# Dynamic convolution and tanh-shrink MLP: first weight tiles staged and cast by ScalarE, start-up taps shared anew, transposes moved

## The chip, the cores and the metric

One core of one Trainium2 chip. The metric is the device time of one execution, in microseconds (us). Every result below is a median of fast runs beside runs of the kernel before on the same chip; those runs of the kernel before had medians of 770.07 to 770.72 us. A span is the time from the first to the last instruction of the profiled execution; it is 1.8 to 2.2 us shorter than the device time. PE is TensorE's matmul pipe, PEld its weight loads, DVE is VectorE, ACT is ScalarE, POOL is GpSimd, SP is SyncE.

## The reference

```python
# x (8, 4096, 192), weight_gen (8, 4096, 8, 7)
w = softmax(weight_gen, axis=-1)                     # 7 taps for each of 8 heads
y[b, s, h, g] = sum_k w[b, s, h, k] * x_pad[b, s + k, h, g]   # x_pad: 6 zero rows ahead of each sequence
hid = y.reshape(32768, 192) @ w_in                   # w_in (192, 2048)
out = (hid - tanh(hid)) @ w_out                      # w_out (2048, 192)
```

## The kernel before

The 32,768 tokens go through in 32 superblocks of 1,024, n = 0 to 31. One superblock passes these hands:

- SP loads its weights (`wg_t`) and its rows of x (`x_t`, with a halo of six rows). There are two buffers for x, so the load of n + 3 can start only when the taps of n + 1 are done.
- ACT takes the exponential, DVE sums and inverts, and the products of x with the seven taps run on GpSimd (`products`). In superblocks 0 and 1, DVE takes four and two of them. An accumulating DMA adds the odd taps onto the even ones.
- PE transposes and sums the products through the identity (`conv`), ACT copies the result out of PSUM as `convT`.
- PE multiplies by `w_in` in 16 f tiles of 128 columns (`gemm1`), ACT takes tanh, DVE subtracts. PE multiplies the superblock before by `w_out` (`gemm2`) between the f tiles.

```python
    for k in range(K):                                    # products(n): taps
        eng, w = (nc.vector, wsm_v) if k in on_vector else (nc.gpsimd, wsm[:])
        eng.tensor_mul(dst[k]..., x_t[:, k : k + J, :]..., w[:, :, :, k : k + 1]...)
        if k == K - 2 and in_pairs:
            nc.gpsimd.dma_start(out=even..., in_=odd..., accum_op=add)
    ...
    load_wg(0); load_x(0); softmax_exp(0); softmax_norm(0, obank[0])
    load_wg(1); load_x(1)
    load_w_in(0, FA)          # GpSimd's DMA casts FP32 to BF16, lower 64 partitions
    products(0, on_vector=(3, 4, 5, 6), ..., hooks={2: rest_of_w_in})
    ...
    copy_w_in(0, FA, nc.scalar)   # to the upper 64 partitions
    copy_w_in(FA, F, nc.sync)
    products(1, on_vector=(0, 1), hooks={4: load_w_out})
    conv(0, (0, 1), (2,))
    load_x(2)
    for n in range(NTOT):
        if n + 3 < NTOT:
            load_wg(n + 3)
            load_x(n + 3)
        for p in range(J):
            gemm1(n, 2 * p); gemm1(n, 2 * p + 1)
            ...
            if n >= 1:
                gemm2((n - 1) * J + p)
            if p == 0 and 1 <= n < NTOT - 2:
                products(n + 2, behind=last_sub[0] if n > 1 else None)
            if n + 1 < NTOT:
                if p == (6 if n > 0 else 7): conv(n + 1, (0, 1))
                if p == (6 if n > 1 else 7): conv(n + 1, (2,))
```

The softmax here doesn't subtract the row's maximum and nothing guards it: scores larger than these inputs give would overflow.

## Time and profile before

770.57 us (770.43 to 771.18), span 768.7.

| kernel before | us |
|---|---|
| GpSimd's first tap of superblock 1 | 20.59 |
| first tanh of n = 0 / 1 / 2 | 22.35 / 45.11 / 71.03 |
| from there to the first tanh of n = 31, a superblock | 22.80 mean, 22.63 median |
| GpSimd's own cycle | 22.64 |
| first tanh of n = 31 / end of the span | 732.28 / 768.73 |

Mean and median of PE's cycle differ because some superblocks have a stall in them. The waits of PE between 74 and 722 us show what kind; the columns are total us, how often, and the longest:

```profile
PE pc L233 <- issue: 2.8, 5, 1.7
PE obank L289 <- issue: 0.8, 1, 0.8
PE ph L257 <- issue: 0.8, 1, 0.8
```

The list has no other line for PE. "issue" means that PE had nothing to execute although nothing that the profile shows held it.

### The profile page before, as it was taken

The page shows a single profiled execution, that of the slowest core. Times are in us where ns is not written, and L with a number is a line of the kernel's source. Part 1 is how long each engine was busy: PE and PEld are TensorE (multiplying, and loading weights), DVE is VectorE, ACT ScalarE, POOL GpSimd, SP SyncE. Part 2 cuts the span into 40 slices and gives each one's busy share as a digit, 9 for nine tenths or more (in the row PEclk, how much of TensorE's full clock was granted, in tenths as well). Part 3 has the DMA queues.
Part 4 walks back from the last instruction along what each step waited for, and adds up shares of the span by engine and source line. Part 5 has one row for each costly group of instructions (what it writes and reads, how often), then busy time and mean ns, then how long its engine had stood idle before and what let it go on. Part 6 is the DMA issues. An engine that isn't in the chain of part 4 may idle for free.

```text
span 768.7 us, 32330 instructions
## 1 busy us (share of the span) xinstructions
PE 736.7 (96%) x14784; PEld 583.1 (76%) x14784; DVE 652.9 (85%) x595; ACT 640.8 (83%) x865; POOL 695.2 (90%) x290
## 2 busy tenths in 40 slices
PE   2799999999999999999999999999999999999997
PEld 2377787777777777788777777777778777787777
DVE  5987888888898888889888888888888988888883
ACT  1777878888888888888888888888888888888883
POOL 5999999999999999999999999999999999999100
PEclk9999999999999999999999999999999999999999
DMA  7823776555677555577655557765556765542412
GB/s 209 184 81 87 182 181 150 118 145 147 169 182 174 131 129 148 150 180 182 164 123 133 150 160 182 180 128 137 143 150 172 182 181 115 125 142 72 98 43 84
DMA packets 25847, 111.37 MB, mean 145 GB/s; under 512 B 4800, under 2 KB 9456, under 8 KB 21624
## 3 DMA queue, kind: packets, MB, share of 16 engines
q1 hardware_dynamic: 14688, 76.95, 29.9%
q0 software_dynamic: 10816, 31.99, 25.8%
q8 instruction: 115, 1.88, 1.0%
q10 hardware_dynamic: 208, 0.39, 0.2%
q14 instruction: 20, 0.16, 0.1%
HBM read 54.49 MB, written 25.17 MB: 104 GB/s over the span
## 4 chain that ended last, share of the span: by engine, by line
PE 93%; DVE 2%; issue 1%; POOL 1%; DMA 1%; ACT 1%; SPq 0%; POOLq 0%
PE ph L257 43%; PE obank L289 43%; PE pc L233 6%; DVE gt L269 2%; PE po L323 1%; DMA x_t<-in_x_dram 1%; POOL even L192 1%; ACT th L267 0%; ACT convT L244 0%; POOL odd L192 0%; DVE zr L151 0%; DVE zsum L145 0%; SPq L117 0%; SPq L93 0%; SPq L121 0%
## 5 line engine op out<-in xcount | busy, mean ns | idle before, releaser
L269 DVE TENSOR_TENSOR gt<-ph,th 128x1024 bf16<-128x1024 f32 x512 | 602.8, 1219 | 93.3 <-ACT th L267 92.7
L267 ACT ACTIVATE th<-ph 128x1024 f32<-128x1024 f32 x512 | 497.2, 1022 | 65.7 <-PE ph L257 64.9
L257 PE MATMUL ph<-convT,w_in 64*128 64x512 bf16 x3072 | 382.1, 378 | 7.5 <-DVE gt L269 5.0
L289 PEld LDWEIGHTS <-gt 64*128 64x128 bf16 x7936 | 345.1, 94 | 53.4 <-issue 2.5
L289 PE MATMUL obank<-w_out,gt 64*128 64x192 bf16 x7936 | 374.6, 243 | 2.9 <-issue 2.1
L192 POOL TENSOR_TENSOR even<-x_t,wsm 128x1536 bf16<-128x1536 f32 x94 | 272.8, 2903 | 3.9 <-DMA x_t<-in_x_dram 1.6
L192 POOL TENSOR_TENSOR odd<-x_t,wsm 128x1536 bf16<-128x1536 f32 x93 | 269.9, 2903 | 0.0
L257 PEld LDWEIGHTS <-w_in 64*128 64x128 bf16 x3072 | 180.1, 94 | 108.4 <-issue 11.8
L192 POOL TENSOR_TENSOR last<-x_t,wsm 128x1536 bf16<-128x1536 f32 x31 | 103.4, 3336 | 0.0
L307 ACT ACTIVATE out_sb<-obank 128x192 f32<-128x192 f32 x248 | 81.9, 330 | 10.5 <-PE obank L289 4.6
L244 ACT ACTIVATE convT<-pc 128x1024 bf16<-128x1024 f32 x64 | 48.9, 808 | 31.6 <-PE pc L233 31.5
L233 PE MATMUL pc<-ident,even 64*128 64x64 bf16 x2304 | 47.9, 192 | 2.9 <-POOL even L192 1.5
L233 PEld LDWEIGHTS <-even 64*128 64x128 bf16 x2304 | 42.7, 96 | 4.1 <-issue 2.2
L201 POOL DMA_DIRECT2D even<-odd x29 | 34.9, 1205 | 9.1 <-POOL odd L192 9.1
L163 POOL TENSOR_TENSOR wsm<-e_t,zr 128x448 f32<-128x448 f32 x30 | 41.7, 1390 | 0.0
L233 PE MATMUL pc<-ident,odd 64*128 64x64 bf16 x448 | 15.5, 198 | 13.1 <-DVE odd L192 12.8
L135 ACT ACTIVATE e_t<-wg_t 128x448 f32<-128x448 f32 x32 | 18.5, 578 | 8.2 <-DMA wg_t<-in_weight_gen_dram 8.2
L233 PE MATMUL pc<-ident,last 64*128 64x64 bf16 x768 | 23.3, 192 | 1.8 <-issue 1.7
L145 DVE TENSOR_REDUCE zsum<-e_t 128x64 f32<-128x448 f32 x32 | 19.5, 609 | 2.9 <-ACT e_t L135 2.9
L233 PEld LDWEIGHTS <-odd 64*128 64x128 bf16 x448 | 11.3, 100 | 13.6 <-DVE odd L192 12.9
L151 DVE RECIPROCAL zr<-zsum 128x64 f32<-128x64 f32 x30 | 16.6, 553 | 3.0
L233 PEld LDWEIGHTS <-last 64*128 64x128 bf16 x768 | 17.0, 96 | 2.2 <-issue 1.8
(20 smaller groups left out, 48.7 us busy)
## 6 DMA issues: line engine op xcount, KB each, us to landing
x_t<-in_x_dram SPq DMA_DIRECT2D x24, 1344.0 KB
even<-odd POOLq DMA_DIRECT2D x29, 1024.0 KB, 8.8
out_dram<-out_sb SPq DMA_DIRECT2D x31, 768.0 KB
x_t<-in_x_dram SPq DMA_DIRECT2D x8, 1176.0 KB
wg_t<-in_weight_gen_dram SPq DMA_DIRECT2D x32, 224.0 KB
x_t<-in_x_dram SPq DMA_DIRECT2D x8, 157.5 KB
w_in<-in_moe_w_in_dram POOLq DMA_DIRECT2D x6, 128.0 KB, 7.5
w_out<-in_moe_w_out_dram POOLq DMA_DIRECT2D x1, 768.0 KB, 10.8
```

The costliest lines, as they stand in the source:

```text
L135: nc.scalar.activation(out=e_t[:].rearrange("p j h k -> p (j h k)"), in_=wg_t[:].rearrange("p j h k -> p (j h k)"), func=ACT.Exp,)
L145: nc.vector.reduce_sum(out=zsum[:], in_=e_t[:].rearrange("p j h k -> p (j h) k"), axis=AX.X)
L163: return eng.tensor_mul(wsm.rearrange("p j h k -> p (j h) k"), e_t[:].rearrange("p j h k -> p (j h) k"), zr.rearrange("p (n o) -> p n o", ...
L192: eng.tensor_mul(dst[k].rearrange("p c j h g -> p j h c g"), x_t[:, k : k + J, :].rearrange("p j (h c g) -> p j h c g", h=H, c=NC), w[:, : ...
L201: nc.gpsimd.dma_start(out=even[:].rearrange("p i c j h g -> p (i c j h g)")[:, 0:ACC], in_=odd[:].rearrange("p i c j h g -> p (i c j h g)" ...
L233: nc.tensor.matmul(pc[:, r, col : col + R], lhsT=prods[c][gi][r * R : (r + 1) * R, c, 2 * j : 2 * j + 2].rearrange("p j h g -> p (j h g)") ...
L244: nc.scalar.activation(out=convT[:, c0 : c0 + nch, :].rearrange("p c (j r t) -> p r (c j) t", r=2, t=R), in_=pc[:, :, 0 : nch * JH * R].re ...
L257: nc.tensor.matmul(ph[:, r, :], lhsT=w_in[r * R : (r + 1) * R, c, f * P : (f + 1) * P], rhs=convT[r * R : (r + 1) * R, c, :], start=(c == ...
L267: last_act[0] = nc.scalar.activation(out=th[:], in_=ph_f, func=ACT.Tanh)
L269: last_sub[0] = nc.vector.tensor_sub(gt[:], ph_f, th[:])
L289: mm = nc.tensor.matmul(po[:, 0:D], lhsT=g_of[n][f][r * R : (r + 1) * R, col : col + P], rhs=w_out[r * R : (r + 1) * R, f, :], start=(r == ...
L307: last_act[0] = nc.scalar.activation(out=out_sb[:, j, :], in_=po[:, 0:D], func=ACT.Copy)
```

## The change

Its intent: start sooner, and let PE's transposes fill holes. It loads the first five f tiles of `w_in` as FP32 into both halves of the partitions and lets ACT cast them. Superblock 0's x comes without its halo first, and GpSimd gets three of its taps (the first of them needs no halo) and DVE four, two of them split so that the positions without halo come first. The scaling of superblock 1's weights moves from DVE to GpSimd, and superblock 2's norm and products go ahead of n = 0. The transposes of 1 sum up in the output banks during n = 0; from n = 1 on, five transposes are mixed behind each f tile of a second matmul, and two f tiles of the next one fill the hole behind them.

```diff
     load_wg(0)
     load_x(0)                       # now rows without halo first, halo after
+    load_wg(1)
     softmax_exp(0)
+    load_wg(2)
+    for c in range(NC):             # FA = 5 * P: 983 KB of FP32, both halves
+        for r in range(2):
+            nc.sync.dma_start(out=w_st[r * R : (r + 1) * R, c, :], in_=w_in_rows(c, 0, FA))
+    load_x(1)
+    load_w_in(FA, FB, last_exp[0])
     softmax_norm(0, obank[0])
-    load_wg(1)
-    load_x(1)
-    load_w_in(0, FA)
-    products(0, on_vector=(3, 4, 5, 6), ...)
+    products(0, taps=[(G_, 6, 0, J), (V, 5, 1, J), (V, 4, 2, J), (V, 5, 0, 1), (V, 4, 0, 2),
+                      (G_, 0, 0, J), (V, 3, 0, J), (V, 2, 0, J), (G_, 1, 0, J)], ...)
     softmax_exp(1)
+    for c in range(NC):
+        nc.scalar.activation(out=w_in[:, c, 0:FA], in_=w_st[:, c, :], func=ACT.Copy)
+    softmax_exp(2)
     ...
-                if p == (6 if n > 0 else 7):
-                    conv(n + 1, (0, 1))
+            if 1 <= n < NTOT - 1 and p == 6:
+                sums = conv_sums(n + 1, ((0, 1),), pcs)
+                gemm2((n - 1) * J + 6, between=lambda f: [next(sums, None) for _ in range(0 if f < LEAD else MIX)])
+                ...
+                gemm2((n - 1) * J + 7, 0, FILL)       # LEAD, MIX, FILL = 6, 5, 2
```

More of the change, by code (lines that the diff above doesn't have):

```diff
@@ L78 @@
     last_sub = {}
-    last_wsm = {}
+    last_exp = {}
     def order(inst, other, reason):
@@ L103, in load_x, with rows @@
         x_t = xpool.tile([P, HALO + J, D], FP32, name="x_t")
-        def rows(p0, p1):
-            win = x[b, s0 + p0 * J - HALO : s0 + p0 * J - HALO + 1]
+        def rows(p0, p1, r0=0, r1=HALO + J):
+            win = x[b, s0 + p0 * J - HALO + r0 : s0 + p0 * J - HALO + r0 + 1]
             nc.sync.dma_start(
-                out=x_t[p0:p1, :, :],
+                out=x_t[p0:p1, r0:r1, :],
                 in_=bass.AP(
@@ L111, in rows, with no_halo @@
                     offset=win.offset,
-                    ap=[[J * D, p1 - p0], [D, HALO + J], [1, D]],
+                    ap=[[J * D, p1 - p0], [D, r1 - r0], [1, D]],
                 ),
             )
-        if s == 0:
+        def no_halo():
             nc.sync.dma_start(
@@ L120, in load_x @@
             )
-            nc.sync.dma_start(
-                out=x_t[0:1, HALO : HALO + J, :],
-                in_=x[b, 0:J].rearrange("(p j) d -> p j d", p=1),
-            )
+        if n == 0:
+            rows(0, P, HALO, HALO + J)
+            rows(16, P, 0, HALO)
+            rows(1, 16, 0, HALO)
+            no_halo()
+        elif s == 0:
+            no_halo()
+            rows(0, 1, HALO, HALO + J)
             rows(1, 16)
@@ L134, in softmax_exp @@
         e_t = wgpool.tile([P, J, H, K], FP32, name="e_t")
-        nc.scalar.activation(
+        last_exp[0] = nc.scalar.activation(
             out=e_t[:].rearrange("p j h k -> p (j h k)"),
@@ L147, in softmax_norm @@
         )
+        zr = wgpool.tile([P, J * H], FP32, name="zr")
         wsm = wgpool.tile([P, J, H, K], FP32, name="wsm")
         if bank is None:
-            zr = wgpool.tile([P, J * H], FP32, name="zr")
             nc.vector.reciprocal(zr[:], zsum[:])
@@ L153, in softmax_norm @@
             return
-        zr = bank[:, 512 - J * H : 512]
-        nc.vector.reciprocal(zr, zsum[:])
+        zr_v = bank[:, 512 - J * H : 512]
         wsm_v = bank[:, 0 : J * H * K].rearrange("p (j h k) -> p j h k", j=J, h=H)
-        scale(nc.vector, wsm_v, e_t, zr)
-        last_wsm[0] = scale(nc.vector, wsm[:], e_t, zr)
-        wsm_of[n] = (wsm, wsm_v, None, None)
+        nc.vector.reciprocal(zr_v, zsum[:])
+        if n == 0:
+            scale(nc.vector, wsm[:], e_t, zr_v)
+        else:
+            nc.vector.tensor_copy(zr[:], zr_v)
+        scale(nc.vector, wsm_v, e_t, zr_v)
+        wsm_of[n] = (wsm, wsm_v, None if n == 0 else e_t, zr)
     def scale(eng, wsm, e_t, zr):
@@ L167, in scale, with products @@
         )
-    def products(n, on_vector=(), sums=None, hooks={}, behind=None):
+    def products(n, taps=None, sums=None, hooks={}, behind=None):
         x_t = x_of.pop(n)
@@ L189, in products @@
             hooks[-1]()
-        for k in range(K):
-            eng, w = (nc.vector, wsm_v) if k in on_vector else (nc.gpsimd, wsm[:])
+        for eng, k, j0, j1 in taps or [(nc.gpsimd, k, 0, J) for k in range(K)]:
+            w = wsm_v if eng is nc.vector else wsm[:]
             eng.tensor_mul(
-                dst[k].rearrange("p c j h g -> p j h c g"),
-                x_t[:, k : k + J, :].rearrange("p j (h c g) -> p j h c g", h=H, c=NC),
-                w[:, :, :, k : k + 1]
+                dst[k][:, :, j0:j1].rearrange("p c j h g -> p j h c g"),
+                x_t[:, k + j0 : k + j1, :].rearrange("p j (h c g) -> p j h c g", h=H, c=NC),
+                w[:, j0:j1, :, k : k + 1]
                 .rearrange("p j h (k o) -> p j h k o", o=1)
-                .to_broadcast([P, J, H, NC, GC]),
+                .to_broadcast([P, j1 - j0, H, NC, GC]),
             )
@@ L215, in products, with conv_sums @@
             prods_of[n] = [[dst[k] for k in (sums or range(K))]] * NC
-    def conv(n, *parts):
+    def conv_sums(n, parts, pcs, home=None):
         prods = prods_of[n]
@@ L221, in conv @@
             conv_of[n] = cpool.tile([P, NC, HT], BF16, name="convT")
-        convT = conv_of[n]
-        pcs = [psum_h.tile([P, 2, HT], FP32, name="pc", tag="ph") for _ in parts]
+        for _ in parts:
+            pcs.append(home or psum_h.tile([P, 2, HT], FP32, name="pc", tag="ph"))
+        if parts[-1][-1] == NC - 1:
+            prods_of.pop(n)
         for gi in range(max(len(g) for g in prods)):
@@ L233, in conv @@
                             nc.tensor.matmul(
-                                pc[:, r, col : col + R],
+                                pc[r][:, col : col + R] if home else pc[:, r, col : col + R],
                                 lhsT=prods[c][gi][
@@ L241, in conv, with conv_out @@
                             )
+                            yield
+    def conv_out(n, parts, pcs):
         for chunks, pc in zip(parts, pcs):
             c0, nch = chunks[0], len(chunks)
-            nc.scalar.activation(
-                out=convT[:, c0 : c0 + nch, :].rearrange("p c (j r t) -> p r (c j) t", r=2, t=R),
-                in_=pc[:, :, 0 : nch * JH * R].rearrange("p r (cj t) -> p r cj t", t=R),
-                func=ACT.Copy,
-            )
-        if parts[-1][-1] == NC - 1:
-            prods_of.pop(n)
+            out = conv_of[n][:, c0 : c0 + nch, :].rearrange("p c (j r t) -> p r (c j) t", r=2, t=R)
+            cols = nch * JH * R
+            if isinstance(pc, list):
+                for r in range(2):
+                    nc.scalar.activation(
+                        out=out[:, r],
+                        in_=pc[r][:, 0:cols].rearrange("p (cj t) -> p cj t", t=R),
+                        func=ACT.Copy,
+                    )
+            else:
+                nc.scalar.activation(
+                    out=out,
+                    in_=pc[:, :, 0:cols].rearrange("p r (cj t) -> p r cj t", t=R),
+                    func=ACT.Copy,
+                )
+    def conv(n, *parts):
+        pcs = []
+        for _ in conv_sums(n, parts, pcs):
+            pass
+        conv_out(n, parts, pcs)
     def gemm1(n, f):
@@ L266, in gemm1 @@
         g1_act[0] = last_act.get(0)
+        gt = gpool.tile([P, TOK], BF16, name=f"gt{f}", tag=f"gt{f}")
         last_act[0] = nc.scalar.activation(out=th[:], in_=ph_f, func=ACT.Tanh)
-        gt = gpool.tile([P, TOK], BF16, name=f"gt{f}", tag=f"gt{f}")
         last_sub[0] = nc.vector.tensor_sub(gt[:], ph_f, th[:])
@@ L272, with gemm2 @@
     LAST = (NTOT - 1) * J
+    LEAD, MIX, FILL = 6, 5, 2
     half = {}
     out_of = {}
-    def gemm2(i):
+    def gemm2(i, f0=0, f1=NFT, between=lambda f: None):
         ops = []
@@ L282, in gemm2 @@
             n, j = divmod(blk, J)
-            if r == 0:
+            if r == 0 and f0 == 0:
                 half[blk] = obank[blk % 2]
             ops.append((r, n, j, half[blk]))
-        for f in range(NFT):
+        for f in range(f0, f1):
             for r, n, j, po in ops:
@@ L299, in gemm2 @@
                     order(mm, g1_act[0] if i == 1 else last_act[0], "row tiles in one bank")
-        if i > 0:
+            between(f)
+        if i > 0 and f1 == NFT:
             blk = i - 1
@@ L350, in load_w_out @@
         nc.gpsimd.dma_start(out=w_out[:], in_=moe_w_out.rearrange("(c p) e -> p c e", c=NFT))
-    FA = 8 * P
-    def load_w_in(f0, f1):
-        for c in range(NC):
-            src = moe_w_in[c * GC : c * GC + 1, f0:f1]
-            dma = nc.gpsimd.dma_start(
-                out=w_in[0:R, c, f0:f1],
-                in_=bass.AP(
-                    tensor=src.tensor, offset=src.offset, ap=[[G * F, H], [F, GC], [1, f1 - f0]]
-                ),
-            )
-            if f0 == 0:
-                order(dma, last_wsm[0], "order of the loads")
@@ L368, in copy_w_in, with w_in_rows, load_w_in @@
-    def copy_w_in(f0, f1, eng):
-        eng.dma_start(out=w_in[R:P, :, f0:f1], in_=w_in[0:R, :, f0:f1])
+    FA, FB = 5 * P, 10 * P
+    w_st = const.tile([P, NC, FA], FP32, name="w_st")
+    def w_in_rows(c, f0, f1):
+        src = moe_w_in[c * GC : c * GC + 1, f0:f1]
+        return bass.AP(
+            tensor=src.tensor, offset=src.offset, ap=[[G * F, H], [F, GC], [1, f1 - f0]]
+        )
+    def load_w_in(f0, f1, behind=None):
+        for c in range(NC):
+            dma = nc.gpsimd.dma_start(out=w_in[0:R, c, f0:f1], in_=w_in_rows(c, f0, f1))
+            if c == 0 and behind is not None:
+                order(dma, behind, "order of the loads")
@@ L371, in rest_of_w_in, with copy_w_in @@
+    def copy_w_in(f0, f1):
+        nc.sync.dma_start(out=w_in[R:P, :, f0:f1], in_=w_in[0:R, :, f0:f1])
     def rest_of_w_in():
-        load_w_in(FA, F)
+        load_w_in(FB, F)
+    V, G_ = nc.vector, nc.gpsimd
     load_wg(0)
     load_x(0)
+    load_wg(1)
     softmax_exp(0)
+    load_wg(2)
+    for c in range(NC):
+        for r in range(2):
+            nc.sync.dma_start(out=w_st[r * R : (r + 1) * R, c, :], in_=w_in_rows(c, 0, FA))
+    load_x(1)
+    load_w_in(FA, FB, last_exp[0])
     softmax_norm(0, obank[0])
-    load_wg(1)
@@ L379 @@
-    load_x(1)
-    load_w_in(0, FA)
     products(
         0,
-        on_vector=(3, 4, 5, 6),
-        sums=(3, 0, 4, 5, 1, 6, 2),
-        hooks={2: rest_of_w_in},
+        taps=[
+            (G_, 6, 0, J),
+            (V, 5, 1, J),
+            (V, 4, 2, J),
+            (V, 5, 0, 1),
+            (V, 4, 0, 2),
+            (G_, 0, 0, J),
+            (V, 3, 0, J),
+            (V, 2, 0, J),
+            (G_, 1, 0, J),
+        ],
+        sums=(6, 5, 4, 3, 0, 2, 1),
+        hooks={1: rest_of_w_in},
@@ L386 @@
     )
     softmax_exp(1)
+    for c in range(NC):
+        nc.scalar.activation(out=w_in[:, c, 0:FA], in_=w_st[:, c, :], func=ACT.Copy)
+    softmax_exp(2)
     softmax_norm(1, obank[1])
-    load_wg(2)
-    copy_w_in(0, FA, nc.scalar)
-    copy_w_in(FA, F, nc.sync)
-    products(1, on_vector=(0, 1), hooks={4: load_w_out})
+    copy_w_in(FA, FB)
+    copy_w_in(FB, F)
+    products(
+        1,
+        taps=[(V, 0, 0, J), (V, 1, 0, J)] + [(G_, k, 0, J) for k in range(2, K)],
+        hooks={4: load_w_out},
+    )
@@ L393, with some @@
+    load_x(2)
+    softmax_norm(2)
+    products(2)
     conv(0, (0, 1), (2,))
-    load_x(2)
+    def some(sums, m):
+        for _ in range(m):
+            next(sums, None)
     for n in range(NTOT):
@@ L401 @@
             gemm1(n, 2 * p + 1)
-            if n == 0 and p == 1:
-                softmax_exp(2)
+            if n == 0:
+                if p == 3:
+                    pcs = []
+                    sums = conv_sums(1, ((0, 1),), pcs, obank)
+                if 3 <= p <= 6:
+                    some(sums, (3 if p == 3 else 1) * 4 * JH)
+                if p == 7:
+                    some(sums, K * 4 * JH)
+                    conv_out(1, ((0, 1),), pcs)
+                    conv(1, (2,))
+                continue
             if p == 5 and n + 3 < NTOT:
                 softmax_exp(n + 3)
-            if n >= 1:
+            if p < 6 or n == NTOT - 1:
                 gemm2((n - 1) * J + p)
-            if p == 0 and 1 <= n < NTOT - 2:
-                products(n + 2, behind=last_sub[0] if n > 1 else None)
-            if n + 1 < NTOT:
-                if p == (6 if n > 0 else 7):
-                    conv(n + 1, (0, 1))
-                if p == (6 if n > 1 else 7):
-                    conv(n + 1, (2,))
-            if n == 0 and p == 2:
-                softmax_norm(2)
-                products(2)
+            if p == 0 and n == 1:
+                softmax_exp(3)
+            if p == 1 and n == 1:
+                softmax_norm(3)
+                products(3)
+            if p == 0 and 1 < n < NTOT - 2:
+                products(n + 2, behind=last_sub[0])
+            if 1 <= n < NTOT - 1 and p == 6:
+                pcs = []
+                sums = conv_sums(n + 1, ((0, 1),), pcs)
+                gemm2(
+                    (n - 1) * J + 6,
+                    between=lambda f: [next(sums, None) for _ in range(0 if f < LEAD else MIX)],
+                )
+                for _ in sums:
+                    pass
+                conv_out(n + 1, ((0, 1),), pcs)
+                conv(n + 1, (2,))
+                gemm2((n - 1) * J + 7, 0, FILL)
             if p == 6 and n + 3 < NTOT:
                 softmax_norm(n + 3)
+            if 1 <= n < NTOT - 1 and p == 7:
+                gemm2((n - 1) * J + 7, FILL, NFT)
     gemm2(LAST)
```

## The prediction

> **What bounds the kernel now.** I first read the page (busy shares, then the chain of work that ended last), then busy time by stage, then the timelines of the start-up, of one steady superblock, and of GpSimd alone. There are 32 superblocks of 1,024 tokens, n = 0 to 31.
>
> ```profile
> PE 736.7 (96%) x14784; PEld 583.1 (76%) x14784; DVE 652.9 (85%) x595; ACT 640.8 (83%) x865; POOL 695.2 (90%) x290
> PE 93%; DVE 2%; issue 1%; POOL 1%; DMA 1%; ACT 1%; SPq 0%; POOLq 0%
> ```
>
> TensorE carries 93% of the chain that sets the end. The stages, cut at 10.3 (first tap), 20.7 (first matmul of n = 0), 44.1 (n = 1), 70.6 (n = 2) and 731.6 (n = 31):
>
> ```profile
> 10.30:20.70 10.40, 5.47 (x168) 4.68 (x169) 10.30 (x9) 1.62 (x3) 10.38 (x7) 1.00 0.74 201
> 20.70:44.10 23.40, 17.55 (x264) 8.97 (x263) 22.59 (x22) 18.31 (x21) 23.30 (x10) 1.00 0.84 206
> 44.10:70.60 26.50, 24.49 (x508) 20.48 (x509) 19.93 (x18) 20.22 (x27) 26.42 (x11) 1.00 0.25 63
> 70.60:731.60 661.00, 656.26 (x13222) 520.94 (x13223) 574.22 (x517) 577.34 (x780) 632.46 (x256) 1.00 0.59 149
> 731.60:768.70 37.10, 32.97 (x624) 28.05 (x620) 23.18 (x26) 21.46 (x35) 0.00 (x0) 1.00 0.17 66
> ```
>
> The busy columns are PE, PEld, DVE, ACT, POOL. Until 44.1 PE is not the limit: DVE and POOL are. In the steady stage PE is 99% busy, but POOL is close behind. The start-up, from the timeline:
>
> ```profile
> 10.28 1.75 DVE L192 TENSOR_TENSOR odd<-x_t,obank 128x1536 bf16<-128x1536 f32 x1 [3.77 <-DMA x_t<-in_x_dram]
> 10.32 2.90 POOL L192 TENSOR_TENSOR even<-x_t,wsm 128x1536 bf16<-128x1536 f32 x1 [1.57 <-DMA x_t<-in_x_dram]
> 18.90 1.70 POOL L358 DMA_DIRECT2D w_in<-in_moe_w_in_dram x3
> 20.59 2.93 POOL L192 TENSOR_TENSOR even<-x_t,wsm 128x1536 bf16<-128x1536 f32 x1
> 23.40 7.21 DVE L269 TENSOR_TENSOR gt<-ph,th 128x1024 bf16<-128x1024 f32 x6 [0.60 <-ACT th L267]
> 36.13 0.97 POOL L163 TENSOR_TENSOR wsm<-e_t,zr 128x448 f32<-128x448 f32 x1
> ```
>
> Both tap engines wait for x of superblock 0 until 10.3, while its weights are ready at 6.5. Then DVE needs 23.4 to 44.1 for the 16 subtractions of n = 0. In the steady state:
>
> ```profile
> 596.59 1.20 POOL L201 DMA_DIRECT2D even<-odd  x1 [0.30 <-POOL odd L192]
> 619.23 1.20 POOL L201 DMA_DIRECT2D even<-odd  x1 [0.30 <-POOL odd L192]
> 613.24 2.36 DVE L269 TENSOR_TENSOR gt<-ph,th 128x1024 bf16<-128x1024 f32 x2 [0.26 <-ACT th L267]
> 613.94 0.88 PE L233 MATMUL pc<-ident,even 64*128 64x64 bf16 x48
> 615.65 1.47 PE L257 MATMUL ph<-convT,w_in 64*128 64x512 bf16 x12
> ```
>
> One POOL cycle is 619.23 - 596.59 = 22.64 us; the PE cycle, from the transposes at 613.94 to those at 636.57, is 22.63. They are equal within the trace. After the transposes, whose issue ends near 615.46, PE waits until 615.65, when DVE's subtraction (to 615.60) frees the PSUM buffer: 0.19 us per superblock. The waits of POOL from 60 to 715 have one entry, its own 0.3 us ahead of the accumulating DMA. So POOL never waits for others: it runs freely at its own limit, and PE at its own.
>
> **What the Trainium skill says.** "GPSIMD Engine Reference", Performance versus the Vector engine, has elementwise work about 2x slower on GpSimd; here a tap costs 2.90 us against 1.75, or 1.66x. "ScalarE: Activation LUTs", What ACT_TABLE_LOAD costs, gives 186 ns + 0.833 ns per element for an activation with immediates; here 448 elements took 578 ns and 1024 took 1022 (559 and 1039 by the formula), so I take 0.73 us as an estimate for 640. "DMA: Bandwidth & Descriptors", Issuing engines are not separate DMA queues, says that all queues share the same 16 engines; the trace shows x of superblock 0 landing 7.3 us after its issue while the loads of w_g and of x of superblock 1 queue behind it. "Runtime: NRT & Kernel Launch", Instruction fetch mechanics, says instructions come in 16 KiB blocks of 256; the page of before has 115 such packets (1.88 MB), as PE's 29,568 instructions need. The chain has PE stalls called "issue" (1.33 us at 66.87, 1.65 at 113.17); that they are late blocks is my guess, since transposes use instructions fastest.
>
> **The change, part by part.**
>
> *Start-up loads.* The halo-free part of x (786 of 1,376 KB) goes first, at about 1.2 us instead of 2.5 to 2.9. In the trace x moves at some 300 GB/s (estimate from packets of 5 to 8.5 us). With data from about 3.2 it lands near 5.9; the halo lands near 8.5. POOL issues three w_in loads behind exp (ends 3.96): to about 6.0, as three took 1.92. The first tap then starts near 6.1, not 10.3.
>
> *Taps of 0.* POOL keeps three: 6.1 + 3 x 2.87 = 14.7; then the rest of w_in (1.7) to 16.4, then the scaling of superblock 1, moved from DVE to POOL (1.05), to 17.45. Its next tap stood at 20.59: POOL gains 3.1 us. DVE's four taps, two of them split, take about 6.8 to 7 us and end near 13.5, if the halo is there by 9.2.
>
> *Price in DMA.* The FP32 staging (983 KB) goes ahead of x of superblock 1. Up to that x about 4.7 MB must pass; at 300 to 390 GB/s it lands at 16.3 to 18. Then DVE does taps 0 and 1 (3.4), norm 2 (1.15), and its first subtraction comes near 21 instead of 23.4.
>
> *Casts.* Three of 0.73 us on ScalarE, while it is idle: hidden. They remove the copy of w_in to the upper half from the path of the first matmul.
>
> *n = 0.* Sixteen subtractions at 1.19 make 19.0 us, now without norms 2 and 3 (2 x 1.1) and without the stall for w_in's second half (1.1 of the 1.74 us hole at 31.1). The transposes of 1 in the output banks no longer take ph buffers. n = 1 starts near 40.3 (44.1 before): 3.8 us gained.
>
> *n = 1.* Before: 26.5, with 1.4 of issue stall and 0.9 of waiting for convT at its end. The convT wait goes; norm 3 comes in and delays a subtraction by about 0.8. I take 24.8, so n = 2 starts at 65.1 (70.6 before).
>
> *Steady state.* Mixing five transposes behind each f removes the 0.19 us wait, since two f of the next block (0.16) fill it, but five is odd, so the two row groups get uneven work; I estimate that this gives back half. PE cycle 22.55. Issue stalls of this stage in before are 661.0 - 29 x 22.63 = 4.7 us; at a slower instruction rate I expect half.
>
> **The sum, for two limits.** PE alone: 65.1 + 29 x 22.55 + 37.1 = 756.2, plus 2.4 of stalls, 758.6. POOL: the last accumulating DMA starts at 710.17 in before; 3.1 earlier is 707.1; it lands 8.8 later (median of the page) at 715.9; from the first transposes that need it to the end is 768.7 - 727.09 = 41.6, plus 0.8 because mixing starts them earlier, less 0.2: 758.1. In before PE had 8 us to spare here (landing 719, transposes at 727.1) and 4 at the first (75.77 + 8.8 against 88.5). The change uses this up: PE gains more than POOL does. With two limits this close I add 0.6. Span 759.2, and 1.8 for time over span (770.52 - 768.7): 761.0.
>
> **Rivals.** *POOL does not bind and the stalls vanish:* PE alone without stalls would be 756.2 + 1.8 = 758. Against it: POOL has no idle time to give, and its work only moves 3 us. For this reason over 2% (under 755.4) is unlikely. *The staged load costs more than it saves:* if x of superblock 1 lands at 20 or later, POOL and DVE both wait there and the gain shrinks to about 3 us: 767. For it: DMA was already near saturation from 4 to 15 us. *Mixing hurts PE:* if uneven row groups cost more than 0.2 us per superblock, the cycle is 22.8 and the time 767 to 768. Against it: 16 matmuls of one row group stand alone at 45.5 in the trace and are spaced 82 ns, as pairs are, so a weight load hides even behind its own row group.
>
> **Range and chances.** The start and POOL's position each carry about 1.5 us, stalls 2. 757.5 to 765.5 should hold 8 times in 10. Faster by over 2%: 0.04; within: 0.95; slower: 0.01.
>
> **What would show it.** Right: first POOL tap near 6; POOL's scaling of superblock 2 near 33 (36.13 before); n = 1 at 39 to 42; POOL still without outside waits to its end near 711; PE waits for the accumulating DMA at the transposes from n = 2 on, with the PE cycle at 22.64. Wrong: a POOL wait for x near 17; more and longer issue stalls; transposes mixed with a cycle over 22.7; or a PE that never waits for POOL and cycles at 22.4.

## More of the kernel before

A useful ruler in all kernels is the first tanh of each superblock on ACT, which marks that PE has done its first f tile. Another is GpSimd's first tap of superblock 1, since from there GpSimd has work without a gap.

## The result, and the profile after

774.51 us (773.42 to 774.98, four runs) against 770.57: ratio 1.0048, 95% interval 1.003 to 1.0065, so 3.9 us slower where 9.5 us faster was predicted. A ratio is the mean time of one kernel's fast runs over that of the other's of the same rounds, so not quite the ratio of the medians. The page's busy shares and chain:

```profile
PE 738.2 (96%) x14784; PEld 578.2 (75%) x14784; DVE 652.7 (84%) x597; ACT 639.0 (83%) x869; POOL 696.3 (90%) x291
PE 93%; DMA 3%; DVE 2%; issue 1%; ACT 0%; SPq 0%; DVEq 0%
```

The busy times have hardly changed, so the 3.9 us are waiting. New in the chain are 3% of DMA. The timeline of the start shows which one (start, duration, engine, line, operation, then idle time before it and what ended it):

```profile
13.03 0.74 ACT L437 ACTIVATE w_in<-w_st 128x640 bf16<-128x640 f32 x1 [3.67 <-DMA w_st<-in_moe_w_in_dram]
16.54 0.74 ACT L437 ACTIVATE w_in<-w_st 128x640 bf16<-128x640 f32 x1 [2.77 <-DMA w_st<-in_moe_w_in_dram]
20.10 0.74 ACT L437 ACTIVATE w_in<-w_st 128x640 bf16<-128x640 f32 x1 [2.82 <-DMA w_st<-in_moe_w_in_dram]
22.27 3.57 PE L286 MATMUL ph<-convT,w_in 64*128 64x512 bf16 x18 [6.45 <-ACT convT L269]
24.40 1.75 DVE L201 TENSOR_TENSOR even<-x_t,obank 128x1536 bf16<-128x1536 f32 x1 [8.94 <-DMA x_t<-in_x_dram]
24.44 2.91 POOL L201 TENSOR_TENSOR even<-x_t,wsm 128x1536 bf16<-128x1536 f32 x1 [6.88 <-DMA x_t<-in_x_dram]
```

The casts last 0.74 us as predicted, but they stand ahead of other work in ACT's program: ACT waits for the staged pieces until 20.10, and only at 21.21 copies `convT` of superblock 0, whose transposes PE had ended at 15.81. Worse, DVE and GpSimd both wait for x of superblock 1 until 24.4. The chain has it as one piece, issued at 9.87:

```profile
9.87 14.44 DMA x_t<-in_x_dram
```

Busy time by stage (PE, PEld, DVE, ACT, POOL with numbers of instructions, then granted clock, DMA share, GB/s):

```profile
6.30:22.30 16.00, 5.23 (x170) 4.65 (x172) 9.02 (x11) 4.25 (x7) 11.26 (x7) 1.00 0.98 208
22.30:47.40 25.10, 18.64 (x264) 9.28 (x264) 22.45 (x20) 17.57 (x20) 22.87 (x10) 0.86 0.74 188
47.40:74.80 27.40, 23.64 (x478) 18.06 (x479) 18.96 (x20) 19.49 (x26) 27.32 (x11) 0.97 0.23 61
74.80:735.00 660.20, 657.86 (x13259) 518.39 (x13257) 576.79 (x519) 574.54 (x783) 632.24 (x256) 1.00 0.59 149
```

From 6.3 to 22.3 the DMA engines look 98% busy and move only 208 GB/s; in the kernel before it was 301 GB/s from 4 to 15 us, at a share of 1.02. The granted clock of 0.86 is 6.8 us at half clock, from 28.6 to 35.4. It can't be what delayed GpSimd's tap at 24.44, which comes before it. In n = 1, PE stands still once for long:

```profile
68.47 0.22 PE L245 MATMUL pc<-ident,odd 64*128 64x64 bf16 x3
72.03 0.24 PE L245 MATMUL pc<-ident,odd 64*128 64x64 bf16 x5 [3.33 <-issue]
```

This stall has a second price. From 73.0 to 76.4 the granted clock is 0.50, which costs some 1.7 us if PE works at half speed (an estimate). The kernels e3, e4 and e5 below, whose stall in n = 1 is also over 3 us, have such a stretch in n = 1 too; the other kernels in the first table below have none there. No run tests this alone.

| us | before | after |
|---|---|---|
| GpSimd's first tap of superblock 1 | 20.59 | 24.44 |
| first tanh of n = 0 / 1 / 2 | 22.35 / 45.11 / 71.03 | 23.76 / 48.35 / 77.59 |
| first tanh n = 2 to n = 31 | 661.25 | 657.83 |
| PE's cycle, median | 22.63 | 22.56 |
| first tanh n = 31 to the end | 36.45 | 37.18 |

By this ruler the change loses 3.2 us up to n = 1 and 3.3 in n = 1, wins 3.4 from there to n = 31 and loses 0.7 at the end. Of these last 0.7 us, 0.6 lie after the last store was issued; this was not pursued. The ruler is true, but as a list of causes it misleads, as the experiments show.

### The profile page after: what moved, and what is told of

It is laid out like the page before. It is cut to its first block, busy times and chain, and to the rows that moved or that the text cites. A ratio compares the mean times of both kernels' runs of the same rounds, so it can differ in the third digit from the quotient of the medians.

```text
span 772.6 us, 32352 instructions
## 1 busy us (share of the span) xinstructions
PE 738.2 (96%) x14784; PEld 578.2 (75%) x14784; DVE 652.7 (84%) x597; ACT 639.0 (83%) x869; POOL 696.3 (90%) x291
## 4 chain that ended last, share of the span: by engine, by line
PE 93%; DMA 3%; DVE 2%; issue 1%; ACT 0%; SPq 0%; DVEq 0%
PE ph L286 43%; PE obank L319 43%; PE pc L245 6%; DMA x_t<-in_x_dram 3%; DVE gt L298 1%; PE po L354 1%; ACT th L297 0%; SPq L414 0%; DVE even L201 0%; DVE odd L201 0%; ACT convT L263 0%; DVE zr L156 0%; DVE zsum L150 0%; SPq L107 0%; SPq L93 0%
## 5 line engine op out<-in xcount | busy, mean ns | idle before, releaser
L319 PE MATMUL obank<-w_out,gt 64*128 64x192 bf16 x7936 | 399.8, 243 | 1.3 <-issue 0.5
L286 PE MATMUL ph<-convT,w_in 64*128 64x512 bf16 x3072 | 386.2, 380 | 12.9 <-ACT convT L269 6.5
L319 PEld LDWEIGHTS <-gt 64*128 64x128 bf16 x7936 | 351.3, 94 | 53.6 <-issue 1.7
L286 PEld LDWEIGHTS <-w_in 64*128 64x128 bf16 x3072 | 176.4, 94 | 118.5 <-issue 27.5
L201 POOL TENSOR_TENSOR last<-x_t,wsm 128x1536 bf16<-128x1536 f32 x32 | 106.3, 3322 | 0.0
L245 PE MATMUL pc<-ident,even 64*128 64x64 bf16 x2256 | 68.6, 191 | 1.3 <-issue 1.0
L245 PEld LDWEIGHTS <-even 64*128 64x128 bf16 x2304 | 64.5, 96 | 1.8 <-issue 1.0
L269 ACT ACTIVATE convT<-pc 128x512 bf16<-128x512 f32 (+1 forms) x63 | 47.7, 805 | 4.5 <-PE pc L245 4.5
L140 ACT ACTIVATE e_t<-wg_t 128x448 f32<-128x448 f32 x32 | 18.5, 577 | 6.2 <-DMA wg_t<-in_weight_gen_dram 6.2
```

Of the source, the lines that this page charges most:

```text
L140: last_exp[0] = nc.scalar.activation(out=e_t[:].rearrange("p j h k -> p (j h k)"), in_=wg_t[:].rearrange("p j h k -> p (j h k)"), func=ACT ...
L201: eng.tensor_mul(dst[k][:, :, j0:j1].rearrange("p c j h g -> p j h c g"), x_t[:, k + j0 : k + j1, :].rearrange("p j (h c g) -> p j h c g", ...
L245: nc.tensor.matmul(pc[r][:, col : col + R] if home else pc[:, r, col : col + R], lhsT=prods[c][gi][r * R : (r + 1) * R, c, 2 * j : 2 * j + ...
L269: nc.scalar.activation(out=out, in_=pc[:, :, 0:cols].rearrange("p r (cj t) -> p r cj t", t=R), func=ACT.Copy,)
L286: nc.tensor.matmul(ph[:, r, :], lhsT=w_in[r * R : (r + 1) * R, c, f * P : (f + 1) * P], rhs=convT[r * R : (r + 1) * R, c, :], start=(c == ...
L319: mm = nc.tensor.matmul(po[:, 0:D], lhsT=g_of[n][f][r * R : (r + 1) * R, col : col + P], rhs=w_out[r * R : (r + 1) * R, f, :], start=(r == ...
```

## The experiments

Fifteen kernels ran; all gave the reference's result except e5, which is wrong.

### First four: the order of the loads, the staging, the steady part, the DMA engines

**e1: x of superblock 1 ahead of the staging.**

```diff
     load_wg(2)
+    load_x(1)
     for c in range(NC):
         for r in range(2): ...                 # staging
-    load_x(1)
```

> The changed kernel with one edit: the load of x of superblock 1 is issued ahead of the six staging loads of w_in instead of behind them. Theory A (the staging loads sit in front of x of superblock 1, and use only 8 of the 16 DMA engines, as the Trainium skill's DMA page says of a transfer whose slowest dim is 8): x of 1 lands near 14 to 15 instead of 24.4, POOL's first tap of superblock 1 starts near 17.5 (24.4 in the changed kernel), the staging then lands near 21 to 22, the first subtraction comes near 24 (28.9) and the time is 766 to 769. Rival B (the added 983 KB of DMA volume alone is the cost, whatever its order): x of 1 comes earlier, but the staging moves back by as much, first matmul after 24, and the time stays above 772.

Measured: 767.65 us, ratio 0.9964 (0.9949 to 0.9979). Neither tap engine waits for x of 1 any more:

```profile
15.36 1.75 DVE L201 TENSOR_TENSOR even<-x_t,obank 128x1536 bf16<-128x1536 f32 x1
17.49 2.90 POOL L201 TENSOR_TENSOR even<-x_t,wsm 128x1536 bf16<-128x1536 f32 x1
```

GpSimd's 17.49 is the 17.45 of the prediction. The last cast now comes at 22.43 and PE's first f tile at 24.6, 3.9 us later than in the kernel before (20.7), and still the time falls by 6.9 us against the changed kernel (6.5 by the two ratios to the kernel before). That is the first hint that PE's start is not what counts.

**e2: no staging, no casts.** The first eight f tiles come by GpSimd's casting DMA and a copy on SP's queue, as nearly in the kernel before.

```diff
-    FA, FB = 5 * P, 10 * P
+    FA, FB = 8 * P, 8 * P
-    (staging loads and casts)
-    load_w_in(FA, FB, last_exp[0])
+    load_w_in(0, FA, last_exp[0])
-    copy_w_in(FA, FB)
+    copy_w_in(0, FA)
```

> The changed kernel with the staging and the ScalarE casts taken out: the first 8 f tiles of w_in come over the GpSimd queue with the cast in the DMA and are copied to the upper half, as in the kernel before; the new order of x, the new taps, the transposes of 1 in the output banks and the mixing stay. Theory A: x of 1 lands near 13 to 14, POOL's scaling of 1 is followed by its tap at 17.5, w_in is ready near 19 to 21, first subtraction 21 to 23, time 762 to 766. Rival B': w_in is then the late one and lands after 23, so that the first subtraction is no earlier than 24.5, time 768 or more. Rival C (the later parts, not the loads, lose the time): time stays at 772 or more.

Measured: 767.14 us, ratio 0.9958 (0.9943 to 0.9973). GpSimd's first tap of 1 comes at 17.56, as expected, but the time misses the expected 762 to 766. PE waits for the copy until 22.74.

**e3: the old start with the new steady part.** The kernel before, with the change's mixed transposes and filler for n >= 1 alone.

> The kernel before with only the steady-state part of the change: transposes of superblocks 2 and later mixed into the second matmul, two f of the next block ahead of the first matmul. Start-up as before. Theory A (start-up loses, steady state gains): PE cycle 22.56 instead of 22.63, issue stalls fewer, time 766 to 768.5. Rival C (mixing costs PE or is paid back by POOL): cycle 22.63 or more, time 770 or more.

Measured: 769.88 us, ratio 0.9992 (0.9976 to 1.0009): nothing, where 766 to 768.5 was expected. The cycle is 22.56 as in the changed kernel, and n = 2 to 31 take 3.5 us less than before. But n = 1 takes 3.1 us more (28.99 against 25.92), with an issue stall of 3.2 us in the transposes of superblock 2, as in the changed kernel.

**e5: the staging from 64 neighbouring rows.** The Trainium skill, "DMA: Bandwidth & Descriptors", Why a DMA increments its semaphore by 16 and not by 1, says that a DMA is split over the largest number up to 16 that divides the outermost dimension on both sides. The staging's source has an outermost dimension of 8 (the heads), and I had missed that. The changed kernel's trace agrees: in each microsecond from 13 to 18 the staging's packets of 2,560 bytes kept 8.3 to 8.4 engines busy (7.3 on average from 9.3 to 18.5). The packets of x of 1 kept 8.0 to 8.1 at work beside them from 12 to 17: half of its 128 large packets were through by 17.8, and the other half ended only from 19.2 to 23.7.

```diff
-            nc.sync.dma_start(out=w_st[r * R : (r + 1) * R, c, :], in_=w_in_rows(c, 0, FA))
+            nc.sync.dma_start(out=w_st[r * R : (r + 1) * R, c, :], in_=moe_w_in[c * R : (c + 1) * R, 0:FA])
```

> The changed kernel, wrong result on purpose: the six staging loads read 64 neighbouring rows of w_in each instead of 8 groups of 8 rows. Bytes, row length, destination and order are the same; only the source's slowest dim is now 64 instead of 8. Theory A (8 engines): about 16 engines are now at work on the staging, it takes 4 to 5 us instead of 9.3, x of 1 lands near 17 to 18.5 instead of 24.4, time 763 to 767. Rival B (volume): staging and x of 1 move at the same pace as in the changed kernel, x of 1 after 22, time 772 or more.

Measured: 771.89 us, ratio 1.0017; the result is wrong. The staging lasts 8.4 us instead of 9.3, though its packets now keep up to 15 engines busy, and x of 1 lands at 22.4 instead of 24.4. The expected 763 to 767 us was missed; a landing after 22 is what the rival had said. Spreading the staging gains 2 us, the order of the loads (e1) 7. The 2 us are not all that loads on half of the engines cost: 113 of the 128 large packets of x of 1 were through by 18.6 us, and the last ended at 21.2, while GpSimd's load of the rest of `w_in` ran (18.2 to 23.2), which has the same outermost dimension of 8 and was not changed. Whether the last packets waited behind it was not tested.

### Next four: two stalls of PE, and where the time does not go

In eight kernels (before, after, e1 to e5 and e7 below) I compared the load of x of superblock 4 with PE's instruction-fetch packets (16 KiB each, a queue of their own in the trace). In each, a fetch packet began within 0.7 us of the end of the load's last large packet. In the changed kernel's DMA view, from 61.5 to 69.6 us there is this one queue and no fetch at all:

```profile
q1 hardware_dynamic: 302, 1.60, 74.7%
```

and in the next 1.2 us (queue, packets, MB, share of 16 engines):

```profile
q8 instruction: 1, 0.02, 5.6%
q1 hardware_dynamic: 14, 0.01, 2.0%
```

The fetch before had been at 60.09, this one began at 69.67, and PE, idle since 68.69, went on 2.4 us after it began. Theory F: the stall is a fetch that waits behind this load.

**e4: the old placing of the transposes with the new start** (`LEAD, MIX, FILL = 16, 0, 0`).

> The changed kernel with the old placing of the transposes in the steady part (none among the second matmul, no filler behind them); its new start is kept. Theory (the steady part gains, the start loses): cycle back to 22.63 us, n=2 to n=31 some 2 to 3.5 us longer, start and n=1 as in the changed kernel: 776 to 778 us. Rival (the mixed transposes also cause the 3.5 us stall of n=1, since e3 had it with the old start): the stall of n=1 falls to about 1.6 us as in the kernel before, which gives the 2 us back: 774 to 775 us.

Measured: 774.33 us, ratio 1.0048 (1.0036 to 1.0061). The cycle is back at 22.63, the stall of n = 1 is there as before (3.4 us), so mixing does not cause it. Yet the total is the changed kernel's: undoing what was worth 1.9 us cost nothing. Both expectations missed: the time is the rival's, but the stall has not shrunk.

**e6: x of superblock 4 loaded after the transposes of 2.**

```diff
-            load_x(n + 3)
+            if n != 1:
+                load_x(n + 3)
...
                 conv_out(n + 1, ((0, 1),), pcs)
-                conv(n + 1, (2,))
+                inst = conv(n + 1, (2,))           # its copy on ACT
+                if n == 1:
+                    load_x(n + 3, behind=inst) # its DMAs depend on inst
```

> The changed kernel with the load of x of superblock 4 held back until the transposes of superblock 2 are done; nothing else. Theory F (the stall of 3.3 us in n=1 is an instruction fetch of TensorE that waits behind this load: in six kernels the fetch began in the very microsecond in which the load ended): the stall of n=1 falls to 1.3 us or less, period of n=1 from 29.2 to about 26.5, total 771.5 to 772.5 us. Rival (the stall comes from the density of the transposes' instructions alone): stall and total unchanged, 774 to 775 us.

Measured: 774.88 us, ratio 1.0054 (1.0041 to 1.0068). Theory F holds at its place: with the load out of the way the same nine microseconds (61.5 to 70.5) have two fetches,

```profile
q8 instruction: 2, 0.03, 1.3%
```

the stall is 0.4 us, and n = 1 takes 24.63 instead of 29.24. PE is 5.7 us ahead at n = 2 (71.87 against 77.59). And the total is the same, where 771.5 to 772.5 was expected. n = 2 to 5 take 25.6, 23.4, 23.7 and 23.5, with a stall in the second matmul behind the load of x of superblock 5 (its last large packet ended at 92.79, the next fetch began at 93.53):

```profile
95.83 0.91 PE L326 MATMUL obank<-w_out,gt 64*128 64x192 bf16 x17 [2.67 <-issue]
```

**e7: a shorter first piece of w_in.** e2 with six f tiles in the first piece and its copy on ACT's queue; **e8** is e7 with e6's edit.

```diff
-    FA, FB = 8 * P, 8 * P
+    FA, FB = 6 * P, 6 * P
...
     softmax_exp(1)
+    copy_w_in(0, FA, nc.scalar)
     softmax_exp(2)
     softmax_norm(1, obank[1])
-    copy_w_in(0, FA)
```

> As e2 (no staging, no casts) with a first chunk of w_in of 6 instead of 8 f tiles, copied to the other half of the partitions over ACT's queue instead of behind the x loads on SP's. Theory (what is left of the start in e2 is the wait for that copy, 22.74 us): first pair of f tiles at 18 to 19.5 us, first tanh of n=1 at 39.5 to 41, 3 to 4 us ahead of e2; the transposes of superblock 2 then fall into the load of x of superblock 4 and stall by 2.5 to 3.5 us instead of 1.1: 764 to 766 us. Rival (GpSimd's products bound it already): no gain over e2's 767.1.

> e7 with the load of x of superblock 4 held back as in e6. Theory F with the theory of the start: 2 us or more below e7, 760 to 763 us. If the start gains but F is wrong: as e7. If GpSimd's products (22.65 us a superblock, free running) take over as the bound: no lower than about 760 either way.

Measured: 767.17 (ratio 0.9956) and 767.29 us (0.9954), both e2's 767.14. The copy still landed at 20.3 (e8) to 21.7 us (e7), so e7 gained only 1 us at n = 0; but e8's first tanh of n = 2 is at 66.51, 2.9 us ahead of e2's, and that too came to nothing: 760 to 763 us was expected of e8.

So I put the two rulers side by side. "Tap" is GpSimd's first tap of superblock 1:

| kernel | tap | first tanh of n = 2 | end of the span | end minus tap |
|---|---|---|---|---|
| before | 20.59 | 71.03 | 768.73 | 748.14 |
| after | 24.44 | 77.59 | 772.60 | 748.16 |
| e1 | 17.49 | 71.89 | 765.54 | 748.05 |
| e2 | 17.56 | 69.40 | 765.17 | 747.61 |
| e3 | 20.23 | 73.55 | 767.86 | 747.63 |
| e4 | 23.35 | 76.67 | 771.97 | 748.62 |
| e5 | 22.42 | 76.62 | 770.11 | 747.69 |
| e6 | 23.60 | 71.87 | 771.57 | 747.97 |
| e7 | 17.65 | 69.05 | 765.37 | 747.72 |
| e8 | 17.54 | 66.51 | 765.17 | 747.63 |

PE's lead over GpSimd at n = 2 differs by 6 us among these kernels. The end does not care: it is GpSimd's first tap plus 747.6 to 748.6. GpSimd never waits for anybody (its only entry from 60 to 715 in the changed kernel's waits is its own gap ahead of the accumulating DMA), and its cycle is 22.64 in all:

```profile
POOL even L210 <- POOL odd L201: 9.1, 29, 0.6
```

Yet PE never waits for GpSimd's products either; it has only issue stalls. Theory C: when PE comes too near to GpSimd, its fetches fall into the load of x, which starts at GpSimd's last tap; the stalls throw it back. GpSimd sets PE's pace through the loads and the fetches, not through the data.

### Last seven: who sets the end, and by which way

**e11: one tap computed twice.** e8 with tap 6 of superblock 2 done twice on GpSimd, 2.9 us that no instruction of PE's first 66 us waits for.

```diff
-    products(2)
+    products(2, taps=[(G_, k, 0, J) for k in range(K)] + [(G_, K - 1, 0, J)])
```

> e8 with one tap of 2.9 us computed twice on GpSimd at the end of superblock 2's products; nothing of TensorE's first 66 us waits for it. Theory P (the end is GpSimd's first tap of superblock 1 plus a constant): 767.3 + 2.9 = 770.2 us. Rival, and the prediction's step (TensorE has 8 us to spare behind GpSimd and is the nearer bound): 767 to 768 us.

Measured: 770.01 us against e8's 767.29: +2.7 by the medians, +3.2 by the spans (768.3 against 765.2). GpSimd's work sets the end; PE had no 8 us to spare.

**e9: every load of x from superblock 4 on after the transposes of its n.** e8 with e6's edit for all n.

```diff
-                if n == 1:
+                if n + 3 < NTOT:
                     load_x(n + 3, behind=inst)
```

> e8 with every load of x from superblock 4 on held back until the transposes of that n are done. The ten kernels so far all end 748 us (747.8 to 748.2) after GpSimd's first tap of superblock 1, with GpSimd never waiting, while their first tanh of n=2 spreads over 6 us against that tap: what TensorE gains it loses again in fetch stalls. Theory C (the stalls come where TensorE runs so far ahead that its fetches meet the load of x, whose start GpSimd's last tap sets; that is how GpSimd holds TensorE): with the loads out of the way few stalls are left, TensorE comes closer to GpSimd's limit, 761 to 764 us. Rival (stalls come anyway, of the density of instructions): as e8, 767 us. If x now comes too late for GpSimd: over 768, with GpSimd waiting for x.

Measured: 761.75 us (761.50 to 761.85), ratio 0.9890 (0.9877 to 0.9903): the best of all, 8.3 us under the kernel before. The end lies 742.0 us behind the tap instead of 748 (my text gave 747.8 to 748.2 for the others; it is 747.6 to 748.6). PE's waits from 60 to 722 us are these two:

```profile
PE pc L249 <- issue: 0.7, 1, 0.7
PE pc L249 <- DMA even<-odd: 0.3, 1, 0.3
```

The stalls are gone, and for the first time PE waits, once, for the accumulating DMA of the products: that is the true limit behind GpSimd, and it lies 6 us further on than PE was ever let.

**e10: a quarter of tap 6 from GpSimd to DVE**, in superblocks 3 to 31, on e8; **e12** is e9 and e10 together.

```diff
+        late[n] = lambda: tap(nc.vector, K - 1, J - 2, J, wsm[:])     # called at p == 3
-        for eng, k, j0, j1 in taps or [(nc.gpsimd, k, 0, J) for k in range(K)]:
+        for eng, k, j0, j1 in taps or [(nc.gpsimd, k, 0, J - 2 if in_pairs and k == K - 1 else J) for k in range(K)]:
```

> e8 with a quarter of tap 6 (two of eight token positions) of superblocks 3 to 31 given from GpSimd to DVE, at a fourth of a block's second matmuls. Theory P (GpSimd's cycle of 22.65 us sets the end, TensorE's of 22.57 does not): GpSimd needs some 0.7 us less a superblock, is then paced by TensorE, its loads move ahead of the transposes, stalls fade after n=5 or so, 760 to 763 us. Rival (TensorE bound, its stalls its own): 767 us or, since DVE takes 0.45 us more a superblock and delays one subtraction, 768 to 775.

> e9 and e10 together. Under theories P and C: 759 to 762 us, TensorE's cycle 22.57 with hardly a stall, not far from its own limit of 66.5 + 29 x 22.57 + 36.5 + 2 = 759.5. If only one of them holds, as the better one of the two.

Measured: 813.44 us (ratio 1.056) and 825.1 (1.070). Both expectations missed. The quarter tap on DVE was to last a quarter of 1.75 us. It lasted 2.32, and PE then waits for the delayed subtraction in every superblock (e10, 100 to 700 us):

```profile
L205 DVE TENSOR_TENSOR last<-x_t,wsm 128x384 bf16<-128x384 f32 x25 | 58.0, 2321 | 0.0
PE ph L299 <- DVE gt L311: 41.1, 25, 2.0
```

The Trainium skill, "SBUF — State Buffer", SBUF: two separate sides, says that a DVE operation with two inputs in SBUF and a GpSimd operation that reads SBUF share a pair of ports that one of them holds for a whole instruction. The start-up taps of DVE have their weights in PSUM (`obank`) and last 1.75 us beside GpSimd; this one read both from SBUF and lasted 2.32. That agrees, but I ran no variant with the weights in PSUM. Neither run says anything for or against theory C, since DVE had become the bound.

**e13, e14, e15: the later loads of x on the changed kernel, on the kernel before, and on e1.** The edit is e9's; in e14 it is the only one, with the load behind that kernel's last `conv` of n >= 1.

> The changed kernel with every load of x from superblock 4 on held back until the transposes of that n are done, as in e9. Theory C: TensorE keeps what it has at n=2 in e6 (first tanh at 71.9): 71.9 + 29 x 22.565 + 37.2 + 2 = 765.5 us, if GpSimd's last accumulating DMA comes in time with a lag of 13.8 us (e9 ran with 11.6); 766 to 767.5 if that wait takes over. Rival (the gain of e9 needs e8's start): 771 or more.

> The kernel before with the same later loads of x, and nothing of the change. Theory C holds for it too: 69.5 + 29 x 22.63 + 36.5 + 1.8 = 764 us, 763.5 to 766. Then the change, compared like with like, is worth nothing or a loss of about 1 us. Rival (in the kernel before stalls are few and its 22.63 is GpSimd's cycle after all): 769 to 770.5 us.

> e1 (x of superblock 1 ahead of the staging) with the later loads of x: 70.4 + 29 x 22.565 + 37.2 + 2 = 764 us, 763 to 765. Below e13 by 1 to 2 us, since TensorE's start is what counts now and not GpSimd's 7 us of head start. If the head start counts in full, 7 us below e13.

| later loads of x on | time | ratio | without them |
|---|---|---|---|
| after (e13) | 767.97 | 0.9965 (0.9953 to 0.9978) | 774.51 |
| before (e14) | 764.65 | 0.9921 (0.9907 to 0.9934) | 770.57 |
| e1 (e15) | 764.50 | 0.9918 (0.9905 to 0.9932) | 767.65 |
| e8 (e9) | 761.75 | 0.9890 (0.9877 to 0.9903) | 767.29 |

All four gain: 3.2 us for e1, 5.5 to 6.5 for the others. e14 runs every superblock from n = 3 on in 22.63 us and has no wait of PE between 74 and 722 us in its list; it is the kernel before with one load moved, at 6.1 us less than the runs beside it. In e13, PE's list has one entry, again the limit itself:

```profile
PE pc L249 <- DMA even<-odd: 0.6, 1, 0.6
```

Its 767.97 is a little above what was expected. e15's time is the expected one; it is 3.5 us under e13, more than the 1 to 2 expected and not 7: once PE is let near GpSimd, the head start of 6.5 us counts only in part, because e15's PE starts late (behind its casts) and becomes the bound; its end lies 744.6 us behind the tap, not 742.

With these loads out of the way in both, the change (e13) is 3.3 us slower than the kernel before (e14), the change with x first (e15) no faster than it, and the change without staging and with a shorter first piece of `w_in` (e9) 2.9 us faster, or 2.4 by the ratios.

## Why the prediction was wrong

*The start, GpSimd's side.* Right: first tap near 6.1 (6.29 measured), three taps to 14.7 (14.86), `w_in`'s DMA to 16.4 (16.56), casts of 0.73 us (0.74), DVE's taps to 13.5 (13.4).

*"Up to that x about 4.7 MB must pass; at 300 to 390 GB/s it lands at 16.3 to 18."* This step failed: it landed at 24.4. The rate was wrong: the engines gave 208 GB/s from 6.3 to 22.3 us at a share of 0.98. (Nor does the early end come out of the sum: 4.7 MB take 15.7 us at 300 GB/s and 12.1 at 390, so if the first gives 18, the second gives 14.4.) That 983 KB stand ahead of x is shown to be the cost (e1 takes the wait away); that the staging sits on half of the engines is 2 us of it (e5); how the rest divides between its volume and the other load on eight engines is not shown. It moved GpSimd's first tap of superblock 1 from the predicted 17.45 to 24.44, which is 7.0 us, and e1, which mends just this, is 6.9 us faster. The prediction had named it as a rival (x at 20 or later, 767 us) but put it outside its range, and its 767 is itself 7.5 us too low. Its own sign of being wrong, a GpSimd wait for x near 17, is in the trace: from 17.56 to 24.44.

*"Casts. ... while it is idle: hidden."* Half right. Their duration is hidden, their waiting is not: the last piece is cast at 20.84, the copy of `convT` starts at 21.21, and PE's first f tile comes at 22.3 instead of 20.7.

*n = 1 at 40.3, 24.8 us long.* The first tanh of n = 1 came at 48.35, where 40.3 means 41.3, so it was 7.1 late. x alone does not explain it: e1, with x in time, has it at 46.21, since its staged pieces land later, and e8, without staging, at 41.69. n = 1 then took 29.2; 3.3 us of it were the fetch stall, and the stretch at half clock behind it is the likely rest. With the load of x of 4 out of the way it took 24.6 (e6), so the size was right for a kernel without the stall.

*Steady state.* PE's cycle of 22.55 was right (22.56), and so was that stalls shrink to about half (2.3 us in the list against 4.4). Mixing did not hurt. But none of this moved the end: e4, without it, is as fast.

*"In before PE had 8 us to spare here ... The change uses this up."* This is the second step that failed, and the deeper one. The limit of the last accumulating DMA is real, and PE reached it in e9 and e13, with the end 742 us behind the tap. But in the kernel before and after, PE was held 6 us short of it by fetch stalls, so the time followed GpSimd alone. The sum should have read: the end of before, moved by what GpSimd's first tap of superblock 1 moves. With the right landing of x that gives 24.44 - 20.59 = +3.85 us; +3.94 was measured. Even with the predicted 17.45 it gives -3.1, about 767.4, which is e1's 767.65. The prediction's 761.0 needed both x in time and PE free to close up. The change with both (e15) is 764.50; e9 is at 761.75, but without the staging that the prediction was about, so that this meets 761.0 is no proof of its sum.

*The sign in the profile that I misread.* I noted that GpSimd "runs freely at its own limit, and PE at its own", that both cycles were equal within the trace (22.64 and 22.63), and that the stalls were probably late blocks of instructions. Two engines at the same speed over 29 superblocks, with one of them losing 4.7 us in stalls, should have raised the question what keeps them together.

What is not settled: how a fetch comes to wait for a load. In the kernel before, 26 of 115 fetch packets started while 12 or more packets of SP's transfers were under way, which is so for 28% of the time, so it is no plain queue. That moving the loads removes the stalls is shown; the way inside the DMA engines is not.

## What to carry to other kernels

Before an engine's idle time is spent in a forecast, find out what kept it from being used already: plot the distance between two free-running engines over the run and test it with one added tap on the suspected pacemaker. Put nothing ahead of the load that the slower engine waits for, and keep large loads away from the densest stretch of TensorE's instructions; here that was one load moved (e14) and worth 6.1 us, where the change without its staging (e2) is worth 3.1. A cast is only hidden if its input is there in time and its engine has nothing behind it that others wait for; this last point is read from the trace, no run tests it alone.

## What the Trainium skill lacked or had wrong

- "Runtime: NRT & Kernel Launch", Instruction fetch mechanics, calls the cost of crossing a block "mostly hidden" and does not connect fetches with a kernel's own loads. Here single issue stalls reach 3.6 us (e5), the fetches behind them meet loads of x, and moving these loads (e9, e13, e14, e15) is worth 3.2 to 6.5 us of about 765.
- The same section gives TensorE's buffer 128 KiB, or 2,048 instructions. In the changed kernel TensorE's last matmul before the stall started at 68.50 us, with 1,729 recorded instructions done and five blocks of 256 fetched, so 449 instructions had come from what was there at the start. If all instructions are in the record, that fits two blocks (512) better than eight; it is an estimate from one trace.
- No page that I found gives the rate that a core's DMA reaches when transfers on all and on half of its engines follow one another: the share was 0.98 at 208 GB/s from 6.3 to 22.3 us, while x of 1 landed 14.4 us after its issue.
